# Attention and ELU network on one core: first-row products joined to the pair's run, and a wider margin in the plan's hops to TensorE

## The chip, the cores and the metric

The kernel runs on one core of a Trainium2 chip. The metric is device time in microseconds; the time before is the median of three runs. One further execution was taken with the hardware profiler, and all rows of the trace come from that one. Engines are named as in the profile: PE is TensorE (PEld its weight loads), DVE is VectorE, ACT is ScalarE, POOL is GpSimd, SP is SyncE, which issues the DMAs.

## The reference

Two stages follow each other. First causal attention for 8 batches of 8 heads, 576 rows and head size 64, with a decay bias from a running sum; then a network of two layers with an ELU between them on the 4608 rows that come out.

```python
scores = scale * q @ k.T                     # per batch and head, 576 x 576
cum = np.cumsum(np.maximum(s, 0.0), axis=-1)
bias = -(cum[:, :, :, None] - cum[:, :, None, :])
scores = np.where(causal, -1e9, scores + np.minimum(bias, 0.0))
attn = softmax(scores)                       # rows, with 1e-9 in the divisor
x = (attn @ v) as (4608, 512)
h = x @ w_in                                 # (4608, 2048)
g = np.where(h > 0.0, h, np.exp(np.minimum(h, 0.0)) - 1.0)
return g @ w_out                             # (4608, 512)
```

## The kernel before, in words

**Precision.** Most products are made from 16-bit halves: a float32 number is split into a high and a low fp16 part, and three of the four products of parts are added. The lines that make the low parts are on DVE or POOL (L1039 for values, L1255 for probabilities, L840 for x, L1676 for the hidden activations; L425 and L426 for the rest of queries and keys). Scores are made in float32 with a second product for the rest (L1176, tiles kh, qs and then k, q).

**Attention.** The rows of a batch are 64 first rows and four blocks of 128. Work goes by batch: rows 0 to 319 of batches 0 to 2 (a special path, `Low`), then batches 3 to 7 whole, then the remaining rows of batches 0 to 2. Within a batch it goes by pair of heads j = 0..3, and each head is a `Unit`. For each block of a head, a score product fills a bank of PSUM (L1176), DVE adds the mask and takes the minimum (L1179), ACT takes the exponential (L1189), and the probabilities are split into halves, written as fp16 and transposed by a DMA into the tile T (`halved`, L1211 to L1260). Batches 4 to 7 have the 64 first rows of both heads of a pair in one tile of probabilities (`early`, L1313 to L1330); their transposed form lies behind the others in T of the second head, and the first 64 values of both heads are put together by two small DMAs (L1043 to L1046).

**The products of values.** `weighing` (L1334) makes, per pair, one plan operation `heads` with 28 products (L1396) into the bank `av`, with the two heads side by side in the two halves of the array (128*64 in the profile). For the pairs with `early` there is a second operation `firsts` (L1407 to L1420) with six products of 64 columns (L1414), also in halves, into a bank `avn`. Both banks are copied to the network's input x by `produce` (L810), a high part on ACT or DVE and a low part on DVE.

**The network.** It goes by chunks of 256 rows, 18 in all. Per chunk there are eight steps; in each, `hidden` makes 24 products of 256 columns (L1636) into a bank h, ACT and DVE make the ELU and its halves (L1654 to L1676), and `project` adds 12 products of 512 columns to two sums o (L1697).

**The order.** Nothing is executed in the order of the source. Each operation is put into a `Plan` with the engines that could do it and a cost for each, a priority, and what it reads and writes. `issue` (L179) then simulates: again and again it takes the operation that can start first, and among those that can start at the same time the one with the smallest priority number; attention has small numbers, network products large ones (10000 and more), so network products fill what attention leaves of PE. The time at which an operation can start is the largest of: its engine is free; its inputs are ready plus a hop between the two engines (`ready`, L172, and the table `HOPS`, for instance 255 ns from DVE to PE and 270 from ACT to PE, 150 where the table has none, as from a DMA); and its new buffers are free (`slot_free` in `issue`, L187 to L193, the end of the last use plus 150). For work of DVE and POOL that uses memory which both read, the plan also keeps the two apart in time (`PORT_LEAD`). The plan's order becomes the program order of each engine; on the chip each engine goes through its instructions in that order and waits on semaphores where the plan's times were not met.

**Banks.** PSUM has eight banks: two for scores (tag a), one for the products of values (av), two for sums o, two for h, and one called third, which serves scores early and h later. A bank asked for by `score_bank` (L1161) belongs to tag a in the order of the source: the n-th such request gets its place in turn. A bank with the tag any and no banks of its own (as in `any_bank`, L627) takes whichever of the others it names is free.

Of the kernel before, what the change touches and what calls it, by code (L numbers as in the profile page):

```python
# [9 lines left out]
F32 = mybir.dt.float32  # L10
# [7 lines left out]
P = 128  # L18
# [9 lines left out]
N_ST, N_A, N_AV, N_H, N_O, N_IO, N_G, N_GG, N_X, N_T, N_K, N_V = 2, 2, 1, 2, 2, 2, 1, 3, 2, 2, 2, 2  # L28
# [26 lines left out]
N_FREE = 0  # L55
N_EARLY, N_AUX, N_URGENT = 2, 4, 1

FILL_T, GAP = 60e3, 350.0

N_FILL = 300  # L60
# [29 lines left out]
class Plan:  # L90
# [14 lines left out]
        ("Pool", "Pool"): 50.0,  # L105
    }
    HOP = 150.0

    BIAS = {"DVE": 1.3, "DVE-SB": 1.3}
    FIRST_BIAS = {"DVE": 1.3, "DVE-SB": 1.3}  # L110
# [21 lines left out]
    def op(self, prio, ways, reads=(), writes=(), late=()):  # L132

        o = Op()
        o.ways, o.prio, o.filler = ways, (prio, len(self.ops)), False
        o.after, o.before, o.behind, o.bufs, o.new = set(late), [], [], set(), []
        firsts = set()
        for accesses, write in ((reads, False), (writes, True)):
            for a in accesses:
                b, part = a if isinstance(a, tuple) else (a, None)  # L140
                if not b.parts and b not in o.bufs:

                    o.new.append((b, self.place(b)))
                    b.first = o
                firsts.add(b.first)
                if b not in o.bufs:
                    o.bufs.add(b)
                    b.users += 1
                for key, (writers, readers) in b.parts.items():
                    if part is None or key is None or key == part:  # L150
                        o.after.update(writers)
                        if write:
                            o.after.update(readers)
                writers, readers = b.parts.setdefault(part, ([], []))
                if write:
                    if part is None:
                        b.parts = {None: ([o], [])}
                    else:
                        b.parts[part] = ([o], [])
                else:  # L160
                    readers.append(o)
        o.after.discard(o)
        firsts -= o.after | {o}
        for d in o.after:
            d.before.append(o)
        for d in firsts:
            d.behind.append(o)
        o.left, o.ready = len(o.after) + len(firsts), {}
        self.ops.append(o)
        return o  # L170

    def ready(self, o, engine):  # L172
        return max(
            (t + (0.0 if e is None else self.HOPS.get((e, engine), self.HOP))
             for e, t in o.ready.items()),
            default=0.0,
        )

    def issue(self):  # L179
        engines = sorted({self.ENGINE.get(w[0], w[0]) for o in self.ops for w in o.ways})  # L180
        port = 0.0
        free = dict.fromkeys(engines, 0.0)
        taken = dict.fromkeys(self.tags, 0)
        slots, skipped = {}, {}
# [2 lines left out]
        def slot_free(key, bufs):  # L187

            held = slots.get(key, ())
            if len(held) < bufs:  # L190
                return 0.0
            was = held[-bufs]
            return None if was.users else was.until + self.HOP  # L193

        pending = [o for o in self.ops if not o.left]
        block = self.nc.cur_bb.bb
        last = {}
        n_done = 0
        while pending:
# [12 lines left out]
            for o in pending:  # L212
                t = 0.0
                for b, k in o.new:
# [13 lines left out]
                    t = max(t, at)  # L228
# [17 lines left out]
            engine, cost, trace = o.ways[n][:3]  # L246
            lag = 0.0
            end = start + cost
            if engine in self.PORT_LEAD:
                port = end  # L250
            engine = self.ENGINE.get(engine, engine)
# [50 lines left out]
def pe16(n):  # L302

    return n / 2.4 + 2.5
# [41 lines left out]
def kernel(  # L346
# [31 lines left out]
    HB = P // 2  # L378
# [7 lines left out]
    ps = ctx.enter_context(tc.tile_pool(name="ps", bufs=1, space=bass.MemoryType.PSUM))  # L386

    plan = Plan(tc)
    op = plan.op
# [771 lines left out]
    def score_bank(name):  # L1161

        return plan.buf(ps, [P, 512], F32, name, tag="a", bufs=N_A, others=[("third", 1, first_stage)], always=True)
# [170 lines left out]
    def weighing(u):  # L1334

        prio = u.prio + 1
        av = plan.buf(ps, [P, 512], F32, f"av_{u.tag}", tag="av", bufs=N_AV)

        def products(cost, pairs, dst, first, last):

            for m, (reads, operands) in enumerate(pairs):
                op(prio, [("PE", cost, lambda m=m, operands=operands: pe_.matmul(
                    av.v[:, dst], *operands(), start=first and m == 0,
                    stop=last and m == len(pairs) - 1))], reads, [av])

        if u.h is None:
            def pair():
                tr = plan.buf(ps, [P, 512], F32, f"tr_{u.tag}", tag="a", bufs=N_A)
                op(prio, [("PE", 111.0, lambda: pe_.transpose(tr.v[:, :P], u.pp.v, ident))],
                   [(u.pp, "data")], [tr])  # L1350
                pieces = split_pt(prio, u.tag, tr, P)
                products(pe(P), [
                    ([pc, u.vs], lambda pc=pc, m=m: (
                        u.vs.v.rearrange("p n a d -> p n (a d)")[:, 0], pc[0].v[:, m]))
                    for m, pc in enumerate(pieces)], slice(P), True, True)
                x = plan.buf(sb, [P, HB], F32, f"xs_{u.tag}", tag="xs")
                for h in range(2):
                    halves(prio, h, HB, (x, h), 0, av, h * HB)
                col = S_GROUP + 2 * groups.index((u.b, False))
                produce(prio, u.j, u.start, HB, lambda: x.v, [x, (scales, col)],  # L1360
                        lambda: scales.v[:, col : col + 1], on_psum=False)

            return [pair]

        if u.h == 0:
            return []
        pair = (u.first_head, u)
        first, last, wq = u.blocks[0], u.last + 1, P * u.n_blocks

        def columns(kb):  # L1370
            i0, half = max(kb - 1, first), kb > first
            return P * (last - i0) - HB * half

        def part(w, kb, m):
            c = columns(kb)
            if kb == last:
                return w.pt.v[:, 0, P - c :]
            end = (1 + (2 * kb + m + 1) * w.n_blocks) * P
            return w.pt.v.rearrange("p u q -> p (u q)")[:, end - c : end]

        def heads():
            terms = [(kb, m, v) for kb in range(last + 1)
                     for m, v in (((0, 0), (1, 0), (0, 1)) if kb < last else ((0, 0), (0, 1)))]
            order, rest = terms[:1], sorted(terms[1:], key=lambda t: -columns(t[0]))
            final = rest.pop(0)
            while rest:
                order.append(rest.pop())
                if rest:
                    order.append(rest.pop(0))
            order.append(final)  # L1390

            def step():
                for n, (kb, m, v) in enumerate(order):
                    dst = slice(wq - columns(kb), wq)
                    for w in pair:
                        pe_.matmul(  # L1396
                            av.v[w.h * HB : (w.h + 1) * HB, dst], w.values.v[:, w.h, kb, v], part(w, kb, m),
                            start=n == 0, stop=n == len(order) - 1,
                        )

            cost = sum((3 if kb < last else 2) * (pe16(columns(kb)) + 4) for kb in range(last + 1))
            op(prio, [("PE", 200 + cost, step)],
               [(w.pt, i) for w in pair for i in u.blocks] + [(u.values, (m, h)) for m in range(2) for h in range(2)],
               [av])
            produce(prio, u.j, u.start + HB * (first == 0), wq, lambda: av.v[:, :wq], [av], 2.0**-15)

        def firsts():  # L1407
            ends = score_bank(f"avn_{u.tag}")

            def step():  # L1410
                for n, (m, v) in enumerate(((0, 0), (1, 0), (0, 1))):
                    turned = u.pt.v[:, 1 + (u.turns[0] - 2 + m) * u.n_blocks]
                    for h in range(2):
                        pe_.matmul(  # L1414
                            ends.v[h * HB : (h + 1) * HB, :HB], u.values.v[:, 0, NQ + 1, v],
                            turned[:, h * HB : (h + 1) * HB], start=n == 0, stop=n == 2,
                        )

            op(prio, [("PE", 240.0, step)], [(u.pt, 0)] + [(u.values, ("first", h)) for h in range(2)], [ends])
            produce(prio, u.j, u.start, HB, lambda: ends.v[:, :HB], [ends], 2.0**-15)  # L1420

        return [heads] + [firsts] * u.early

    def halves(prio, h, n, dst, c0, av, a0):

# [416 lines left out]
```

## Time and profile before

| what | value |
|---|---|
| median of 3 runs | 1038.01 us (1037.63 to 1040.27) |
| profiled execution | 1035.61 us |
| its span, first to last instruction | 1033.7 us |
| granted TensorE clock | 1.000 |
| busy PE, DVE, ACT, POOL | 1014.4, 834.6, 627.0, 386.1 us |
| PE, two largest groups | L1697 378.7 us (1608 products), L1636 376.0 us (3072) |

The share of busy time says how full an engine is, not how dense: the ends of products are modelled, and a product is drawn longer than the distance to the next one. A row of the waits has the waiting engine and line, the line waited for, microseconds in total, times, and the longest. A row of the timeline has the start, the length, engine and line, what is written from what, the shape, the count, and in brackets the idle time before it and who ended it. A row of the groups has busy microseconds and the mean of one in ns behind the count. A row of the stretches has the window, its length, and busy microseconds with counts for the engines in turn.

### The profile page before, as it was taken

Reading aid. Unit: us, or ns where it says so; the run is one execution under the profiler, and the core shown is the slowest. Engines: PE = TensorE matmul, PEld = TensorE weight load, DVE = VectorE, ACT = ScalarE, POOL = GpSimd, SP = SyncE. Lnnn points to the kernel's source line nnn. Section 1 sums busy time; section 2 is a strip of 40 time slices with the busy share of each in tenths; the row PEclk is TensorE's granted clock in tenths of the full one; section 3 lists DMA queues with packets and bytes.
Section 4 is the critical chain, followed back from the end, with each engine's and each line's share of the span. In section 5 each row is a group of like instructions: output and inputs, shape, how many; then the busy total and the mean of one; then the engine's idle time right before and its main releaser. Section 6 shows DMA issues by size and latency. Waiting matters only on the chain.

```text
span 1033.7 us, 21490 instructions
## 1 busy us (share of the span) xinstructions
PE 1014.4 (98%) x7260; PEld 695.7 (67%) x7260; DVE 834.6 (81%) x2047; ACT 627.0 (61%) x1502; POOL 386.1 (37%) x605
## 2 busy tenths in 40 slices
PE   8999999999999999999999999999999999999998
PEld 6666766667676666676666666666676766676665
DVE  6889899999989999898899998888888888433333
ACT  4877756676666666766676666756666656333232
POOL 6332345464554445547556444423232322000000
PEclk9999999999999999999999999999999999999999
DMA  7767243779668677766787657747464544100000
GB/s 222 233 198 234 62 142 96 175 155 217 130 146 172 131 151 152 186 149 142 162 201 146 148 132 172 151 109 181 112 141 101 129 110 122 34 22 22 1 21 21
DMA packets 277693, 137.73 MB, mean 133 GB/s; under 512 B 211640, under 2 KB 254928, under 8 KB 277584
## 3 DMA queue, kind: packets, MB, share of 16 engines
q1 hardware_dynamic: 277584, 136.37, 54.8%
q8 instruction: 57, 0.93, 0.4%
q14 instruction: 52, 0.43, 0.1%
HBM read 68.63 MB, written 9.88 MB: 76 GB/s over the span
## 4 chain that ended last, share of the span: by engine, by line
PE 84%; DVE 9%; issue 3%; DMA 2%; ACT 1%; POOL 0%; SPq 0%; DVEq 0%; ACTq 0%; POOLq 0%
PE h L1636 30%; PE o L1697 30%; PE sc L1176 10%; PE av L1396 5%; PE o L1603 3%; PE h L1573 3%; DVE p L1255 2%; DVE v L1039 1%; DMA stk<-in_kT_dram 1%; PE trl L975 1%; PE avl L991 1%; DVE p L1179 1%; PE scratch L1760 1%; DVE g L1663 1%; DMA vs<-in_vb_dram 1%
## 5 line engine op out<-in xcount | busy, mean ns | idle before, releaser
L1697 PE MATMUL o<-wp,gg 128*128 128x512 f16 x1608 | 378.7, 380 | 1.0 <-DVE gg L1676 0.8
L1636 PE MATMUL h<-x,wp 128*128 128x256 f16 x3072 | 376.0, 273 | 0.0
L1636 PEld LDWEIGHTS <-wp 128*128 128x128 f16 x3216 | 301.8, 98 | 65.4 <-issue 8.4
L1697 PEld LDWEIGHTS <-gg 128*128 128x128 f16 x1608 | 151.3, 98 | 158.0 <-issue 3.9
L1255 DVE SCALAR_TENSOR_TENSOR p<-p,sm,p 128x512 f16<-128x512 f32 (+3 forms) x234 | 181.1, 789 | 5.3 <-POOL p L1247 2.4
L1189 ACT ACTIVATE p<-p,mn 128x192 f32<-128x192 f32 (+1 forms) x232 | 143.4, 619 | 43.8 <-DVE mn L1179 41.8
L1654 ACT ACTIVATE g<-h,cs 128x512 f32<-128x512 f32 x134 | 91.7, 684 | 111.5 <-PE h L1636 109.2
L1671 ACT ACTIVATE gg<-h,wc 128x512 f16<-128x512 f32 x122 | 83.6, 685 | 96.7 <-DVE h L1667 96.0
L1179 DVE CUSTOM_DVE_ANT_0 p<-sc,maskw 128x192 f32<-128x192 f32 (+1 forms) x232 | 109.2, 477 | 17.4 <-PE sc L1176 14.1
L1676 DVE SCALAR_TENSOR_TENSOR gg<-h,wc,gg 128x512 f16<-128x512 f32 x134 | 99.8, 745 | 25.8 <-ACT gg L1671 25.1
L1176 PE MATMUL sc<-kh,qs 128*128 128x192 f32 (+2 forms) x272 | 109.1, 405 | 7.0 <-DVE mn L1179 5.6
L1247 POOL TENSOR_SCALAR p<-p,sm 128x512 f16<-128x512 f32 (+3 forms) x105 | 61.1, 586 | 145.4 <-DVE sm L1198 104.0
L1667 DVE SCALAR_TENSOR_TENSOR h<-g,cs,h 128x512 f32<-128x512 f32 x134 | 100.6, 751 | 16.2 <-ACT g L1659 12.1
L1663 DVE TENSOR_SCALAR g<-g 128x512 f32<-128x512 f32 x77 | 37.2, 483 | 74.4 <-ACT g L1654 74.1
L1251 ACT ACTIVATE p<-p,sm 128x512 f16<-128x512 f32 (+3 forms) x114 | 67.6, 603 | 32.4 <-DVE sm L1198 30.9
L1176 PE MATMUL sc<-k,q 128*128 128x192 f32 (+2 forms) x272 | 83.2, 309 | 0.0
L1176 PEld LDWEIGHTS sc<-kh,qs 128*128 128x128 f32 x272 | 51.4, 189 | 28.4 <-DVE mn L1179 7.3
L426 POOL TENSOR_TENSOR qs<-stq,qs 64x512 fp32r<-64x512 f32 (+1 forms) x53 | 63.5, 1198 | 6.7 <-ACT qs L407 1.2
L426 POOL TENSOR_TENSOR k<-stk,kh 64x576 fp32r<-64x576 f32 x36 | 54.8, 1523 | 15.3 <-ACT kh L407 11.8
L1396 PE MATMUL av<-T,v 128*64 128x256 f16 (+5 forms) x896 | 60.3, 286 | 0.0
L405 POOL TENSOR_SCALAR qs<-stq 128x512 fp32r<-128x512 f32 (+1 forms) x42 | 27.9, 664 | 72.9 <-DMA stq<-in_qT_dram 51.6
L1176 PEld LDWEIGHTS sc<-k,q 128*128 128x128 f32 x272 | 51.8, 190 | 1.9
(216 smaller groups left out, 1326.1 us busy)
## 6 DMA issues: line engine op xcount, KB each, us to landing
stk<-in_kT_dram SPq DMA_DIRECT2D x64, 288.0 KB
va<-in_vb_dram SPq DMA_DIRECT2D x32, 320.0 KB
stq<-in_qT_dram SPq DMA_DIRECT2D x40, 256.0 KB
w_raw<-in_w_in_dram SPq DMA_DIRECT2D x16, 512.0 KB
w_raw<-in_w_out_dram SPq DMA_DIRECT2D x16, 512.0 KB
out_dram<-ost SPq DMA_DIRECT2D x32, 256.0 KB
q<-qs SPq DMA_DIRECT2D x40, 128.0 KB
T<-p SPq DMA_TRANSPOSE x208
```

Source lines behind the costliest of these rows:

```text
L426: ("Pool", pool_2(n), lambda: pool.tensor_tensor(dst(), src(), hi(), ALU.subtract)),
L1176: pe_.matmul(view(sc.v[:, :cw]), l, r, start=n == 0, stop=n == len(pairs) - 1)
L1179: op(prio, [("DVE", 84 + dve_p(cw), lambda i=i, sc=sc: dve.tensor_tensor_reduce(pt.v[:, i * cw : (i + 1) * cw], sc.v[:, :cw], mv(i * cw, c ...
L1189: op(prio, [("ACT", 480 + w / 1.2, lambda: act.activation(pt.v[:, :w], pt.v[:, :w], AF.Exp, bias=mn.v[:, at : at + 1], scale=-1.0, accum_o ...
L1255: ("DVE-SB", dve_2(n), lambda part=part: dve.scalar_tensor_tensor(part(t16, 1), own(part), by(part), part(t16, 0), ALU.mult, ALU.subtract)),
L1396: pe_.matmul(av.v[w.h * HB : (w.h + 1) * HB, dst], w.values.v[:, w.h, kb, v], part(w, kb, m), start=n == 0, stop=n == len(order) - 1,)
L1636: pe_.matmul(hp.v[:, m], weight_part(f, 0, part)[1]()[:, c * P : (c + 1) * P], x.v[:, xx, c, o : o + TC], start=(c == 0 and i == 0), stop= ...
L1654: op(side, [("ACT", act_c(2 * TC) + 90, lambda: act.activation(gt.v, flat(hp.v), AF.Exp, scale=by(BACK)))], [hp, (cs[ch], g)], [gt])
L1667: op(side, [("DVE", dve_b(2 * TC), lambda: dve.scalar_tensor_tensor(flat(hp.v), gt.v, by(MINUS if sign[0] else FIRST), flat(hp.v), ALU.mul ...
L1671: ("ACT", act_c(2 * TC) + 90, lambda: act.activation(flat(gg.v[:, 0]), flat(hp.v), AF.Copy, scale=down())),
L1676: op(side, [("DVE", dve_b(2 * TC), lambda: dve.scalar_tensor_tensor(flat(gg.v[:, 1]), flat(hp.v), down(), flat(gg.v[:, 0]), ALU.mult, ALU. ...
L1697: pe_.matmul(acc[i].v, gg.v[:, a, m, i * P : (i + 1) * P], weight_part(2 * fp + m, 1, part)[1](), start=(first and m == 0 and k == 0), sto ...
```

## The change

Two things are changed. `firsts` is no operation of its own any more: for the pairs that have it, its six products are the first products of the operation `heads`, which now also reads the first values and opens the bank `ends`; the plan's cost goes from 200 to 350 ns more than the sum of its products. The bank `ends` is asked for with the tag any, and so takes a score bank when one is free, outside the order of the tag a. The other change is in the plan: once its time for PE is past 250e3 ns, `more()` adds 800 ns to each hop from another engine to PE in `ready`, and to the release of every buffer, for any engine, in `slot_free`.

```diff
+MORE_T = 250e3
...
+    MORE = 800.0
...
     def ready(self, o, engine):
+        more = self.more() if engine == "PE" else 0.0
         return max(
-            (t + (0.0 if e is None else self.HOPS.get((e, engine), self.HOP))
+            (t + (0.0 if e is None else self.HOPS.get((e, engine), self.HOP) + more * (e != "PE"))
              for e, t in o.ready.items()),
             default=0.0,
         )
 
+    def more(self):
+        return self.MORE if self.now > MORE_T else 0.0
...
-            return None if was.users else was.until + self.HOP
+            return None if was.users else was.until + self.HOP + self.more()
...
-        def firsts():
-            ends = score_bank(f"avn_{u.tag}")
-
-            def step():
+            def first_rows():
                 for n, (m, v) in enumerate(((0, 0), (1, 0), (0, 1))):
...
-            op(prio, [("PE", 240.0, step)], [(u.pt, 0)] + [(u.values, ("first", h)) for h in range(2)], [ends])
-            produce(prio, u.j, u.start, HB, lambda: ends.v[:, :HB], [ends], 2.0**-15)
-
-        return [heads] + [firsts] * u.early
+            cost = sum((3 if kb < last else 2) * (pe16(columns(kb)) + 4) for kb in range(last + 1))
+            reads = [(w.pt, i) for w in pair for i in u.blocks]
+            reads += [(u.values, (m, h)) for m in range(2) for h in range(2)]
+            if not u.early:
+                op(prio, [("PE", 200 + cost, step)], reads, [av])
+            else:
+                ends = plan.buf(ps, [P, 512], F32, f"avn_{u.tag}", tag="any", bufs=0, others=[("a", N_A)], always=True)
+                op(prio, [("PE", 350 + cost, lambda: (first_rows(), step()))],
+                   reads + [(u.values, ("first", h)) for h in range(2)], [av, ends])
+                produce(prio, u.j, u.start, HB, lambda: ends.v[:, :HB], [ends], 2.0**-15)
+            produce(prio, u.j, u.start + HB * (first == 0), wq, lambda: av.v[:, :wq], [av], 2.0**-15)
+
+        return [heads]
```

More of the change, by code (lines that the diff above doesn't have):

```diff
@@ L177, in ready @@
         )
+    def more(self):
+        return self.MORE if self.now > MORE_T else 0.0
     def issue(self):
         engines = sorted({self.ENGINE.get(w[0], w[0]) for o in self.ops for w in o.ways})
-        port = 0.0
+        port = self.now = 0.0
         free = dict.fromkeys(engines, 0.0)
@@ L1399, in step @@
                         )
[L1401 to L1405, printed above, removed]
-        def firsts():
-            ends = score_bank(f"avn_{u.tag}")
-            def step():
+            def first_rows():
                 for n, (m, v) in enumerate(((0, 0), (1, 0), (0, 1))):
```

## The prediction

> **What bounds the kernel now.** I read the page first, its busy table and its forty slices.
>
> ```profile
> span 1033.7 us, 21490 instructions
> PE 1014.4 (98%) x7260; PEld 695.7 (67%) x7260; DVE 834.6 (81%) x2047; ACT 627.0 (61%) x1502; POOL 386.1 (37%) x605
> ...
> PE   8999999999999999999999999999999999999998
> ...
> DVE  6889899999989999898899998888888888433333
> ```
>
> TensorE is busy from end to end, so only what TensorE itself saves can move the end. VectorE is nearly full while attention and network run together and half empty in the last six slices, where only the network is left. Next come the stretches. The columns after the window are the busy microseconds of PE, PEld, DVE, ACT and POOL.
>
> ```profile
> 250.00:900.00 650.00, 641.82 (x4883) 440.51 (x4881) 563.55 (x1387) 414.25 (x990) 274.24 (x398) 1.00 0.63 142
> 900.00:1025.00 125.00, 125.00 (x866) 84.54 (x865) 45.75 (x70) 39.65 (x60) 0.00 (x0) 1.00 0.04 14
> ```
>
> Behind 900 us PE has no gap at all. Between 250 and 900 us, the stretch that the change's threshold (250e3 ns of the plan's own time) opens, PE has 650.0 - 641.8 = 8.2 us of visible gaps. The waits of that stretch name them.
>
> ```profile
> PE sc L1176 <- DVE mn L1179: 5.6, 9, 1.3
> PE sc L1176 <- DVE x L840: 1.3, 1, 1.3
> PE o L1697 <- DVE gg L1676: 0.8, 1, 0.8
> PE peaks L649 <- DVE tops L641: 0.3, 1, 0.3
> ```
>
> Twelve waits, 5.6 + 1.3 + 0.8 + 0.3 = 8.0 us, all for VectorE, and ten of them are a score product that waits until VectorE has read an older score bank. This is not the whole price, because the end of a product in the trace is modelled and lies behind the start of the next one:
>
> ```profile
> L1636 PE MATMUL h<-x,wp 128*128 128x256 f16 x3072 | 376.0, 273 | 0.0
> ...
> 947.34 5.24 PE h L1636 x48
> ```
>
> One hidden product is drawn 0.273 us long, but in a dense run 48 of them take 5.24 us, 0.109 us each. A wait must therefore first use up 0.273 - 0.109 = 0.16 us before a gap shows. Twelve waits hide another 12 x 0.16 = 1.9 us, so waits for other engines cost about 10 us in this stretch, some 1% of the span. That is all the wider margin can win.
>
> **The change, first part: the sixteen separate visits for the first rows.** The products of `firsts` use two halves of the array (128*64), as those of `heads` do; everything around them uses the whole array (128*128). The timeline of PE shows what such a visit costs.
>
> ```profile
> L1414 PE MATMUL avn<-T,v 128*64 128x64 f16 x96 | 4.5, 203 | 0.0
> ...
> 437.44 1.04 PE L1697 MATMUL o<-wp,gg 128*128 128x512 f16 x4 [0.83 <-DVE gg L1676]
> 438.41 0.28 PE L1414 MATMUL avn<-T,v 128*64 128x64 f16 x6
> 438.62 0.47 PE L1176 MATMUL sc<-kh,qs 128*128 128x448 f32 x1
> 438.93 0.37 PE L1176 MATMUL sc<-k,q 128*128 128x448 f32 x1
> 439.14 1.47 PE L1697 MATMUL o<-wp,gg 128*128 128x512 f16 x6
> 440.44 1.15 PE L1636 MATMUL h<-x,wp 128*128 128x256 f16 x9
> 441.34 0.38 PE L1176 MATMUL sc<-kh,qs 128*128 128x288 f32 x1
> 441.56 0.29 PE L1176 MATMUL sc<-k,q 128*128 128x288 f32 x1
> 441.69 0.30 PE L1176 MATMUL sc<-kh,qs 128*128 128x288 f32 x1
> 441.82 0.29 PE L1176 MATMUL sc<-k,q 128*128 128x288 f32 x1
> 441.96 1.81 PE L1636 MATMUL h<-x,wp 128*128 128x256 f16 x15
> ```
>
> There are 96 / 6 = 16 visits. The `o` product takes (440.44 - 439.14) / 6 = 0.217 us. Four of them from 437.44 end at 438.31, and the next `o` starts at 439.14, so visit and score pair together take 0.83 us. A score pair without a visit: nine `h` from 440.44 end at 441.42, the next `h` starts at 441.96, so two pairs of 288 columns take 0.54 us, 0.47 ns per column and product. The pair of 448 columns is thus worth 2 x 448 x 0.47 = 0.42 us, and 0.83 - 0.42 = 0.41 us is the visit. Its own work is three pairs of 64 columns side by side, at 0.217 / 512 us a column 3 x 0.027 = 0.08 us. So 0.33 us is the way into the half-array form and out of it. One visit had hidden products behind it instead of scores:
>
> ```profile
> 461.95 1.36 PE L1636 MATMUL h<-x,wp 128*128 128x256 f16 x11
> 463.24 0.28 PE L1414 MATMUL avn<-T,v 128*64 128x64 f16 x6
> 463.46 0.83 PE L1636 MATMUL h<-x,wp 128*128 128x256 f16 x6
> ```
>
> Eleven `h` end at 463.15, the next starts at 463.46: 0.31 us, of it 0.23 us of way in and out. In the timeline of all sixteen, fifteen have a score pair right behind. Inside the run of `heads` the six products need no way of their own, since that run pays it already. So the merge saves 15 x 0.33 + 0.23 = 5.2 us, at least 16 x 0.23 = 3.7 us if scores come to stand behind the longer run more often than now. It adds no product, no copy and no DMA. What it adds is conditions: the run now also waits for the two small copies of the first values and for a free score bank, and holds that bank about 2 us longer. Neither is a wait on PE if the plan knows of it, since the plan puts network products first. If the cover failed, one such wait costs what a score wait costs, up to 1.5 us.
>
> **Second part: 800 ns more from other engines to PE, and on every reuse of a buffer, in the plan.** This changes no instruction, only the order. A score pair that the plan thought ready at T is now put on PE at T + 800 or later, and network products go ahead of it. To see what that is worth, take one of the long waits, with VectorE's and GpSimd's rows.
>
> ```profile
> 498.80 2.72 DVE L1039 SCALAR_TENSOR_TENSOR v<-va,scales,v 128x320 f16<-128x320 f32 x2
> ...
> 501.44 0.61 DVE L1179 CUSTOM_DVE_ANT_0 p<-sc,maskw 128x448 f32<-128x448 f32 x1
> ...
> 499.63 1.53 POOL L426 TENSOR_TENSOR k<-stk,kh 64x576 fp32r<-64x576 f32 x1
> ...
> 502.11 0.40 PE L1176 MATMUL sc<-kh,qs 128*128 128x288 f32 x1 [1.27 <-DVE mn L1179]
> ...
> L1039 DVE SCALAR_TENSOR_TENSOR v<-va,scales,v x47: 536/594/1691, 273.5 to 866.8; 128x320 f16<-128x320 f32 x47
> ```
>
> Two L1039 took 2.72 us where twice the median is 2 x 0.594 = 1.19 us: VectorE came 1.5 us late while GpSimd's L426 ran beside it, the score reduction queued behind came late by that, and PE waited 1.27 + 0.16 = 1.43 us. The lateness is VectorE's, and a margin of 0.8 us on PE does not remove it; it covers 0.8 of the 1.43. The Trainium skill (SBUF — State Buffer, section Who interferes with whom) goes further: a VectorE instruction with two SBUF inputs and a GpSimd instruction that reads SBUF exclude each other for the whole of the instruction that came first. By that rule such collisions stay as long as they are however PE is ordered, and the margin would win at most 0.8 us from each; the stretch from 1.19 to 2.72 us agrees with it in kind.
>
> Of the waits, 0.8 us goes from each, or the whole where it is shorter. In the timeline four are about as long as the longest shown, 1.3 + 0.16 = 1.46 us, with 0.66 left each, and the `o` wait at 0.99 with 0.19 left: 4 x 0.66 + 0.2 = 2.8 us left, and 10 - 2.8 = 7 us gone. Bounds: 10 us if all go, and a loss of the same size if the new order brings as many waits again. I take 5.8 us: nearer to the 7, because the wait of the row above is of the kind that the 0.8 shortens, and a little under it, because a new order will have some stalls of its own. Who pays for the later scores: the score banks stand free longer, and attention may fall behind; network products fill PE meanwhile, as they do in the stretch behind 900 us with no gap.
>
> Sum: 5.2 + 5.8 = 11.0 us. The profiled execution took 1035.6 us (span 1033.7 and 1.9 around it), which would become 1024.6. The median of the runs lies 2.4 us above the profiled one, so for it 1038.0 - 11.0 = 1027.0 us. A measurement of this kernel can tell about 0.3%, 3.1 us, from no change.
>
> **Rivals.** First, only the merge works: VectorE's lateness is not noise around the plan but accumulates, PE catches up with it whatever head start it gives, and the waits come back at the same sum. For it speaks that the four long waits are all past 0.8 us; against it, that VectorE has 650 - 563.6 = 86 us idle in the stretch to recover in. Time: 1038.0 - 5.2 = 1032.8 us.
>
> Second, slower: new collisions. The margin is also on every buffer's release, so the plan puts work of ScalarE, VectorE and GpSimd up to 0.8 us later than it can really start. They run ahead of the plan, and GpSimd's L426 meets VectorE's instructions where the plan had held them apart.
>
> ```profile
> L1255 DVE SCALAR_TENSOR_TENSOR p<-p,sm,p x203: 268/742/1894, 254.4 to 891.3; 128x512 f16<-128x512 f32 x58, 128x256 f16<-128x256 f32 x16, 128x384 f16<-128x384 f32 x14, 128x64 f16<-128x64 f32 x14
> ```
>
> L1255 shows the size: up to 1.89 us, 1.15 above its median. The place is 375 to 650 us, where the long waits are. It decides when the waits grow by more than the merge's 5.2 us, that is by four waits of 1.46 us; if they double, 10 - 5.2 = 4.8 us is lost: 1042.8 us. Against it: the margin itself covers 0.8 of each.
>
> Third, the gains cancel: the merged run's added conditions hold it and the scores behind it, and some four waits of 1.3 us eat the merge while the margin wins nothing: 1038.0 us.
>
> Fourth, attention becomes the bound and the network runs out of rows.
>
> ```profile
> L1176 PE MATMUL sc<-kh,qs x233: 252/392/559, 250.5 to 880.8; 128*128 128x288 f32 x57, 128*128 128x448 f32 x28, 128*128 128x320 f32 x16, 128*128 128x192 f32 x16
> ...
> 900.00:1033.70 133.70, 66.64 (x576) 0.00 (x0) 36.91 (x49) 32.64 (x49) 1.00 0.05 17
> ```
>
> The second row is the tile h alone: 576 products, three chunks of 192, are still to do when attention is over, some 130 us. If every one of the 233 score pairs lost 0.8 us on its bank, two banks would lose 233 x 0.8 / 2 = 93 us. That is less than the cushion, so this needs a second delay; I give it no time of its own beyond the second rival's and put it with it.
>
> **How the numbers follow.** Both parts work: 0.60, 1027.0 us, between 1021 and 1031. Only the merge: 0.17, 1032.8 us. Cancelled: 0.10, 1038.0. Slower by new waits or by starving: 0.13, 1042.8. Faster by over 0.3% takes the first two less a hundredth: 0.76; within 0.3% gets that and the third: 0.11; slower 0.13. The range goes down to all waits gone with the merge at its best and 2 us for fewer score pairs behind half-array runs, 1038 - 5.2 - 10 - 2 = 1021, and up to 1037, which leaves out the slower case and part of the cancelled one.
>
> **What would show it.** Right: the first-row products follow or precede `av` products with no whole-array product between them, and visits into the half-array form between 250 and 900 us fall from 45 to 29; PE's gaps there fall from 8.2 to about 3 us; the waits of scores for L1179 fall from nine to four or fewer, each under 0.7 us; the last score pair starts between 880 and 920 us. The order up to about 250 us stays as it is. Wrong: gaps of PE at 8 us or more, above all with more long L1255 or L1039 rows at them; a network product that waits for an `x` tile; or half-array visits as many as before.

## The result and the profile after

| | before | after |
|---|---|---|
| median | 1037.82 us (1035.50 to 1040.27, 4 runs) | 1020.55 us (1019.64 to 1022.21, 4 runs) |
| profiled execution, span | 1035.61, 1033.7 us | 1020.64, 1018.7 us |
| ratio, 95% interval | | 0.9835 (0.9809 to 0.9861) |

The changed kernel is 17.3 us faster where 11.0 were forecast, and 1020.55 lies just under the low end of the range, 1021.0. The direction was right, the size was not. In the new file the line numbers of the score part are higher by 8 (L1176 is L1184, L1179 is L1187, L1255 is L1263); the value products are L1404 and the first-row products L1413.

The page of the changed kernel, with the busy table and the chain by engine:

```profile
span 1018.7 us, 21522 instructions
PE 1006.9 (99%) x7260; PEld 696.9 (68%) x7260; DVE 817.3 (80%) x2044; ACT 618.8 (61%) x1497; POOL 396.3 (39%) x607
...
PE 90%; DVE 4%; DMA 2%; issue 2%; SPq 1%; ACT 0%; POOL 0%; DVEq 0%; ACTq 0%; POOLq 0%
```

PE makes the same 7260 products in 15 us less span. On the chain VectorE has 4%; the same line of the page before is

```profile
PE 84%; DVE 9%; issue 3%; DMA 2%; ACT 1%; POOL 0%; SPq 0%; DVEq 0%; ACTq 0%; POOLq 0%
```

The stretches after (busy PE, PEld, DVE, ACT, POOL behind the window's length):

```profile
0.00:250.00 250.00, 243.05 (x1499) 169.22 (x1500) 223.19 (x588) 173.67 (x456) 110.73 (x205) 1.00 0.62 171
250.00:900.00 650.00, 649.79 (x4987) 451.78 (x4987) 549.40 (x1387) 413.11 (x995) 285.59 (x402) 1.00 0.64 144
```

Between 250 and 900 us PE's gaps fell from 8.2 to 0.2 us, and 4987 products start there instead of 4883. The view of PE's waits for this window has no row left; before it had four. Ahead of 250 us nothing was won: the order of PE first differs at 238 us.

Here is one of the sixteen runs that now begin with the first rows:

```profile
338.81 1.67 PE L1705 MATMUL o<-wp,gg 128*128 128x512 f16 x7
340.41 0.28 PE L1413 MATMUL avn<-T,v 128*64 128x64 f16 x6
340.53 2.10 PE L1404 MATMUL av<-T,v 128*64 128x512 f16 x28
342.56 0.42 PE L1184 MATMUL sc<-kh,qs 128*128 128x320 f32 x1
342.81 0.31 PE L1184 MATMUL sc<-k,q 128*128 128x320 f32 x1
342.96 0.28 PE L1644 MATMUL h<-x,wp 128*128 128x256 f16 x1
```

The six products need 340.53 - 340.41 = 0.12 us and have no way in or out of their own; before, a visit took 0.31 to 0.41 us. And here is a place where VectorE comes late and PE does not notice, from the timelines of VectorE, GpSimd and PE:

```profile
452.25 2.20 DVE L1047 SCALAR_TENSOR_TENSOR v<-va,scales,v 128x320 f16<-128x320 f32 x2
454.38 0.74 DVE L1263 SCALAR_TENSOR_TENSOR p<-p,sm,p 128x512 f16<-128x512 f32 x1
...
455.12 0.47 DVE L1187 CUSTOM_DVE_ANT_0 p<-sc,maskw 128x320 f32<-128x320 f32 x1
...
452.24 1.40 POOL L434 TENSOR_TENSOR k<-stk,kh 64x576 fp32r<-64x576 f32 x1
...
453.65 0.45 PE L1184 MATMUL sc<-kh,qs 128*128 128x448 f32 x1
453.94 0.37 PE L1184 MATMUL sc<-k,q 128*128 128x448 f32 x1
454.15 2.76 PE L1705 MATMUL o<-wp,gg 128*128 128x512 f16 x12
456.56 0.48 PE L1184 MATMUL sc<-kh,qs 128*128 128x288 f32 x1
```

The two value splits (L1047) took 2.20 us beside GpSimd's L434, where two at the median of this line, 0.545 us, take 1.09, as at 498 us before. But the next score pair that needs a bank stands behind a whole group of 12 network products, and the bank was read by 455.6, about 1 us ahead of it.

For the tables below I also worked out waits that the gaps hide: from the starts of the products in the timeline, each distance between network products less what the products in between take in dense runs, and less the usual way into and out of the half-array form; what is left over 60 ns counts as a wait. By that, the kernel before has 18 waits with 12.3 us between 250 and 900 us, and the changed one 3 with 1.1 us. These figures depend a little on what is taken as dense, by some tenths of a microsecond and a few short waits in each run.

### The profile page after: what moved, and what is told of

It is laid out like the page before. It is cut to its first block, busy times and chain, and to the rows that moved or that the text cites. A ratio compares the mean times of both kernels' runs of the same rounds, so it can differ in the third digit from the quotient of the medians.

```text
span 1018.7 us, 21522 instructions
## 1 busy us (share of the span) xinstructions
PE 1006.9 (99%) x7260; PEld 696.9 (68%) x7260; DVE 817.3 (80%) x2044; ACT 618.8 (61%) x1497; POOL 396.3 (39%) x607
## 4 chain that ended last, share of the span: by engine, by line
PE 90%; DVE 4%; DMA 2%; issue 2%; SPq 1%; ACT 0%; POOL 0%; DVEq 0%; ACTq 0%; POOLq 0%
PE o L1705 33%; PE h L1644 33%; PE sc L1184 10%; PE av L1404 5%; PE o L1611 3%; PE h L1581 3%; PE trl L983 1%; PE avl L999 1%; DVE p L1263 1%; SPq L401 1%; DMA kl<-in_kT_dram 1%; DMA vs<-in_vb_dram 0%; DMA w_raw<-in_w_out_dram 0%; DMA aux_dram<-aux 0%; PE sc_n L1330 0%
## 5 line engine op out<-in xcount | busy, mean ns | idle before, releaser
L1263 DVE SCALAR_TENSOR_TENSOR p<-p,sm,p 128x512 f16<-128x512 f32 (+3 forms) x237 | 173.4, 747 | 8.3 <-POOL p L1255 5.4
L1255 POOL TENSOR_SCALAR p<-p,sm 128x512 f16<-128x512 f32 (+3 forms) x130 | 83.6, 648 | 183.7 <-DVE sm L1206 154.6
L1187 DVE CUSTOM_DVE_ANT_0 p<-sc,maskw 128x192 f32<-128x192 f32 (+1 forms) x232 | 109.2, 478 | 23.1 <-PE sc L1184 21.8
L1184 PE MATMUL sc<-kh,qs 128*128 128x192 f32 (+2 forms) x272 | 112.8, 417 | 0.2
L1184 PE MATMUL sc<-k,q 128*128 128x192 f32 (+2 forms) x272 | 83.0, 309 | 0.0
L1259 ACT ACTIVATE p<-p,sm 128x512 f16<-128x512 f32 (+3 forms) x95 | 56.6, 603 | 34.9 <-DVE sm L1206 30.4
L1184 PEld LDWEIGHTS sc<-kh,qs 128*128 128x128 f32 x272 | 51.5, 189 | 20.0 <-issue 3.7
L434 POOL TENSOR_TENSOR qs<-stq,qs 64x512 fp32r<-64x512 f32 (+1 forms) x50 | 59.8, 1196 | 12.6 <-ACT qs L415 5.9
L1404 PE MATMUL av<-T,v 128*64 128x256 f16 (+5 forms) x896 | 60.2, 285 | 0.0
L434 POOL TENSOR_TENSOR k<-stk,kh 64x576 fp32r<-64x576 f32 x34 | 51.2, 1506 | 18.1 <-ACT kh L415 15.3
L1184 PEld LDWEIGHTS sc<-k,q 128*128 128x128 f32 x272 | 51.9, 191 | 2.6
L1404 PEld LDWEIGHTS <-v 128*64 128x64 f16 x896 | 40.1, 110 | 14.8 <-issue 4.9
```

Of the source, the lines that this page charges most:

```text
L434: ("Pool", pool_2(n), lambda: pool.tensor_tensor(dst(), src(), hi(), ALU.subtract)),
L1184: pe_.matmul(view(sc.v[:, :cw]), l, r, start=n == 0, stop=n == len(pairs) - 1)
L1187: op(prio, [("DVE", 84 + dve_p(cw), lambda i=i, sc=sc: dve.tensor_tensor_reduce(pt.v[:, i * cw : (i + 1) * cw], sc.v[:, :cw], mv(i * cw, c ...
L1263: ("DVE-SB", dve_2(n), lambda part=part: dve.scalar_tensor_tensor(part(t16, 1), own(part), by(part), part(t16, 0), ALU.mult, ALU.subtract)),
L1404: pe_.matmul(av.v[w.h * HB : (w.h + 1) * HB, dst], w.values.v[:, w.h, kb, v], part(w, kb, m), start=n == 0, stop=n == len(order) - 1,)
```

## The experiments

All ratios are against the kernel before on the same chip, with 95% intervals; the clock granted was 0.996 to 1.000 in every run. PE busy and waits are of the stretch from 250 to 900 us in the profiled execution of each.

| run | median us | ratio | PE busy of 650 us | waits, us (count) |
|---|---|---|---|---|
| before | 1036.55, 1037.10, 1037.34 (beside e1 to e4, e5 to e8, e9 to e11) | | 641.82 | 12.3 (18) |
| changed | 1020.55 | 0.9835 (0.9809 to 0.9861) | 649.79 | 1.1 (3) |
| e1, merge only | 1031.19 | 0.9942 (0.9927 to 0.9956) | 642.71 | 11.9 (22) |
| e2, margin only | 1025.60 | 0.9891 (0.9873 to 0.9908) | 649.87 | 0.8 (2) |
| e3, hops only | 1029.90 | 0.9936 (0.9920 to 0.9951) | 646.54 | 8.7 (25) |
| e4, release only | 1020.19 | 0.9834 (0.9818 to 0.9850) | 649.94 | 0.3 (1) |
| e5, score banks only | 1021.09 | 0.9845 (0.9831 to 0.9858) | 647.91 | 3.1 (5) |
| e6, 400 ns | 1022.01 | 0.9864 (0.9844 to 0.9885) | 646.52 | 7.0 (13) |
| e7, 1600 ns | 1021.46 | 0.9840 (0.9824 to 0.9857) | 650.00 | 0.4 (2) |
| e8, from the start | 1027.32 | 0.9904 (0.9890 to 0.9917) | 648.46 | 2.6 (5) |
| e9, before, no separation | 1057.86 | 1.0194 (1.0180 to 1.0208) | 635.19 | 23.8 (40) |
| e10, changed, no separation | 1041.82 | 1.0041 (1.0026 to 1.0056) | 643.46 | 13.1 (26) |
| e11, 1200 ns from 170 us | 1018.50 | 0.9820 (0.9806 to 0.9835) | 650.00 | 0.0 |

**The two parts alone.** The first question was whether the two parts bring their gains apart. The merge alone has the margin at zero:

```diff
-    MORE = 800.0
+    MORE = 0.0
```

> The merge alone, the margin set to 0. Theory A (two separate gains: the merge takes away sixteen ways into and out of the half-array form, the margin covers VectorE's lateness): half-array visits fall by 16, worth 4.7 us by the two traces, and PE's waits for VectorE stay at some 10 us; 5 us faster than before, ratio 0.995. Rival C (the waits came from the separate operation, whose score bank was bound to its place in the order of the banks): the waits go with the merge; 12 us or more faster, ratio 0.988.

The margin alone is the kernel before with the lines of `ready`, `more` and `slot_free` of the change.

> The margin alone, on the kernel before with its separate first-row operations. Theory A: 48 half-array visits as before, the waits for VectorE almost gone; 10 us faster, ratio 0.990. Rival C: the waits stay, 5 us or less faster, ratio 0.995.

Both came out by theory A. Visits into the half-array form between 250 and 900 us are 29 in e1 and 45 in e2, as in the kernel before (the expectation has 48 for that). The merge alone wins 0.58% (6.0 us of 1036.55, interval 4.6 to 7.6), the margin alone 1.09% (11.3 us, 9.5 to 13.2), and 0.9942 x 0.9891 = 0.9834 is the ratio of both together. So they add up, and rival C falls: with the merge alone the waits stay. PE's waits in e1 show one thing more:

```profile
PE sc L1184 <- DVE mn L1187: 3.1, 7, 0.8
PE avn L1413 <- DVE mn L1187: 2.5, 3, 1.2
PE h L1644 <- DVE gg L1684: 0.8, 1, 0.8
```

Three of the joined runs wait for a score bank, 2.5 us together. This is the added condition that the prediction named (its third rival); it is real, and the margin covers it, since the changed kernel has no such row.

**Which half of the margin.** Hops to PE alone, and release of buffers alone, both with the merge:

```diff
-            return None if was.users else was.until + self.HOP + self.more()
+            return None if was.users else was.until + self.HOP
```

> The changed kernel with the margin on the hops to PE alone, none on the release of buffers. Nearly all waits of the kernel before are scores that wait for L1179 to have read an older score bank, which is a release and not a hop. Theory A therefore expects the waits to stay at 8 us or more: 5 to 7 us faster than before, ratio 0.994. If the hops matter, the waits are gone and it is as fast as the changed kernel, ratio 0.984.

```diff
-            (t + (0.0 if e is None else self.HOPS.get((e, engine), self.HOP) + more * (e != "PE"))
+            (t + (0.0 if e is None else self.HOPS.get((e, engine), self.HOP))
```

> The changed kernel with the margin on the release of buffers alone, none on the hops to PE. Theory A: as fast as the changed kernel within 2 us, ratio 0.985 to 0.987, with waits of scores for L1179 under 2 us in all. If the hops matter as much, the waits are half of before: ratio 0.990.

The hops bring nothing that can be measured beside the merge (0.9936 against 0.9942), though waits in their trace are a little shorter, and the release brings all of it. The next run narrows it to the two score banks:

```diff
-            return None if was.users else was.until + self.HOP + self.more()
+            return None if was.users else was.until + self.HOP + self.more() * (key[1] == "a")
```

with the hops as in e4.

> The changed kernel with the margin on the release of the two score banks alone: no other bank, no buffer in SBUF, no hop. Theory A1 (the waits are scores that come too early for the bank that VectorE still reads): as fast as the changed kernel within 3 us, ratio 0.984 to 0.987, waits of scores under 2 us. Rival (the release of buffers in SBUF reorders ScalarE, VectorE, GpSimd and the DMAs, and that makes the difference): the waits stay above 5 us, ratio 0.992.

With the two score banks alone the gain is there within the interval, 0.9845 against 0.9834. What is left is mostly a single wait of another bank, and nothing of it concerns SBUF:

```profile
PE h L1644 <- DVE gg L1684: 1.4, 1, 1.4
PE sc L1184 <- DVE mn L1187: 0.7, 2, 0.4
```

**The size.** 

```diff
-    MORE = 800.0
+    MORE = 400.0
```

> The changed kernel with 400 instead of 800 ns. The rule of the prediction (each wait is shortened by the margin and no more): the waits of the merge alone, 22 of some 12 us in all, keep 12 - 22 x 0.4 at the most, 4 to 6 us; ratio 0.988. Rival (the later place also lies behind whole network products, so more than the margin is covered): 1 to 3 us of waits left, ratio 0.985 to 0.986.

The ratio, 0.9864, lies between what the two expected, and its interval holds both; the waits of the profiled execution, 7.0 us, lie above both, but that execution took 1027.1 us, 5 us over the median of its kernel. That 400 ns covers only a part is seen in that one execution; by the medians it is not shown, since the interval overlaps that of 800 ns. With `MORE = 1600.0`:

> The changed kernel with 1600 instead of 800 ns. If 800 already covers all waits: as fast as the changed kernel, ratio 0.983 to 0.985, since the 130 us of network behind the last scores hide a slower attention. If attention becomes the bound: the last scores come later than 1000 us and the time rises above 1025 us, ratio over 0.988.

No gap of PE is left (650.00 of 650 us), and the time is that of the changed kernel. Attention is indeed slower; its last score product starts at 914 us, 50 us later than that of the changed kernel, and the network behind it hides that. First the changed kernel, then e7:

```profile
863.90 0.29 PE L1184 MATMUL sc<-k,q 128*128 128x288 f32 x1
...
914.23 0.29 PE L1184 MATMUL sc<-k,q 128*128 128x288 f32 x1
```

**The place.** With `MORE_T = 0.0`:

> The changed kernel with the margin from the start and not from 250e3 ns. Theory A: ahead of 170 us there are too few network products to put ahead of a score, PE must wait for the chain of attention anyway, and a margin only sends the chain through later: no gain, within 3 us of the changed kernel or slower by up to 10, ratio 0.983 to 0.995. Rival: the waits of the first stage are lateness too and go: 5 us or more faster than the changed kernel, ratio 0.979 or less.

By the two ratios (0.9904 and 0.9835) it is about 7 us slower than the changed kernel, in the way that theory A described. PE's groups show where most of it went: into filler products (L1768, an identity turned over so that PE is not idle), which the plan puts where it finds nothing else in the first 60 us. In e8 they are

```profile
L1768 PE MATMUL scratch<-ident 128*128 128x128 f32 x138 | 20.4, 293 | 0.0
```

and in the changed kernel

```profile
L1768 PE MATMUL scratch<-ident 128*128 128x128 f32 x86 | 14.4, 314 | 0.0
```

52 more at the dense distance of 0.109 us are 5.7 us, which is most of the difference. In the first 60 us only 39 products of the network are made in the changed kernel, and 32 in e8: there is little to put ahead of a score, and the margin becomes idle time.

**The source of the lateness.** To see whether the waits come from VectorE meeting GpSimd, the plan's separation of the two was taken away, in both kernels:

```diff
-    PORT_LEAD = {"DVE-SB": 240.0, "Pool": 120.0}
+    PORT_LEAD = {}
```

> The kernel before with the plan's separation of VectorE and GpSimd (PORT_LEAD) emptied, so that the two meet more often. Theory (the waits are VectorE's lateness from meeting GpSimd): VectorE's busy time between 250 and 900 us grows by 15 us or more, PE's waits there from 12 to 18 us or more; 5 to 15 us slower than before, ratio 1.005 to 1.015. If the lateness has another source: busy time and waits as before, ratio 1.000.

> The changed kernel with the same separation emptied. Theory (the margin does not stop the meetings, it covers the lateness): VectorE's busy time grows as in the run beside it, but PE's waits between 250 and 900 us stay under 5 us; within 8 us of the changed kernel, of which what lies ahead of 250 us is shared with the run beside it, ratio 0.985 to 0.992. If the margin worked by fewer meetings: the waits come back, ratio over 0.995.

The first 250 us of the kernel before, then the two stretches of the same kernel without the separation:

```profile
0.00:250.00 250.00, 243.50 (x1498) 169.02 (x1499) 224.32 (x589) 172.12 (x452) 111.89 (x208) 1.00 0.62 172
...
0.00:250.00 250.00, 236.78 (x1424) 162.14 (x1426) 221.03 (x562) 163.91 (x435) 122.24 (x221) 1.00 0.60 169
250.00:900.00 650.00, 635.19 (x4791) 430.74 (x4785) 578.42 (x1399) 389.67 (x938) 345.67 (x472) 1.00 0.64 144
```

Between 250 and 900 us VectorE is busy 14.9 us longer (578.4 against 563.6), and the waits double, from 12.3 to 23.8 us. That fits lateness from such meetings, but the plan also gave GpSimd more work (345.7 us against 274.2), so it is no pure test. The time rose by more than expected (ratio 1.0194, not up to 1.015), and part of that was lost ahead of 250 us, where 1424 products start instead of 1498. The expectation for e10 failed: its waits are 13.1 us and not under 5, and its ratio, 1.0041, lies where the rival (fewer meetings) had put it. It is 16.0 us faster than e9, nearly the 17.3 us by which the changed kernel beats the one before. The change thus takes away about 11 us of waits in either case (23.8 - 13.1 = 10.7, 12.3 - 1.1 = 11.2), and where there is twice the lateness the rest stays.

So e10 leaves the rival standing. It is answered by e4, whose VectorE rows have instructions as stretched as before while PE is busy 649.94 of 650 us:

```profile
L1263 DVE SCALAR_TENSOR_TENSOR p<-p,sm,p x201: 268/745/1897, 253.4 to 868.0; 128x512 f16<-128x512 f32 x58, 128x384 f16<-128x384 f32 x17, 128x256 f16<-128x256 f32 x14, 128x64 f16<-128x64 f32 x12
L1047 DVE SCALAR_TENSOR_TENSOR v<-va,scales,v x51: 532/547/1694, 251.0 to 846.2; 128x320 f16<-128x320 f32 x51
```

The longest are 1.90 and 1.69 us, before 1.89 and 1.69. The longest alone do not say how many there are. So here is a count, for each trace, of all VectorE instructions between 250 and 900 us that took over 0.8 us more than the fastest tenth of the same operation, tiles and shape in all thirteen traces; I take such an instruction as a sign of a meeting.

| | before | changed | e1 | e3 | e4 | e11 | e9 | e10 |
|---|---|---|---|---|---|---|---|---|
| stretched instructions | 28 | 21 | 30 | 24 | 25 | 30 | 39 | 44 |
| PE's waits, us | 12.3 | 1.1 | 11.9 | 8.7 | 0.3 | 0.0 | 23.8 | 13.1 |

The runs e3 and e4 have as many stretched instructions, and 8.7 and 0.3 us of waits; e11 has about as many as the kernel before, and no wait. Fewer meetings are thus not what took the waits away. In e9 and e10, where the separation is gone, there are 11 and 23 more than in the same kernel with it.

**A faster version.** The last run has 1200 ns from 170 us on:

```diff
-MORE_T = 250e3
+MORE_T = 170e3
...
-    MORE = 800.0
+    MORE = 1200.0
```

> The changed kernel with a margin of 1200 ns from 170e3 ns on, an attempt at a faster version: behind 250 us the changed kernel has 1.1 us of waits left, between 170 and 250 us about 1 us. Theory: at most 2 us to win, ratio 0.981 to 0.984. If the network at 170 to 250 us has too few products to put ahead: slower than the changed kernel, ratio over 0.986.

It has no wait left behind 250 us and the lowest median of all, 1018.50 us. Its interval (0.9806 to 0.9835) overlaps that of the changed kernel, so 1 to 2 us better is likely and not shown.

## Why the prediction was wrong in size

**The bound held.** PE sets the end, and what was won are PE's waits and its ways into and out of the half-array form. Less work on another engine alone moved nothing: in e1 VectorE is busy 551.2 us in the stretch instead of 563.6, and PE's waits stay at 11.9 us.

**The merge** was forecast at 5.2 us, at least 3.7; alone it measured 6.0 (4.6 to 7.6). The half-array visits fell from 45 to 29, as said. The Trainium skill (TensorEngine Tiling (Array Packing), section Key Properties) states that a change of the tiling mode drains TensorE; the 0.23 and 0.33 us around six products agree with a price per change and not per product, since the six add only about 0.1 us inside the run of `heads`.

**The margin** was forecast at 5.8 us and measured 11.3 (9.5 to 13.2). This is the step that failed, in three places of the same sum. First, "waits for other engines cost about 10 us": I added 0.16 us to each of the twelve gaps that show. That is right between two network products, but a score product starts 0.03 us behind the start of a network product in dense runs, so more is hidden: the waits that show as 1.27 us at 502.11 and 1.30 us at 489.33 are 1.52 and 1.65 us by the starts. And waits under some 0.3 us leave almost no gap or none, since the product before is drawn over them. By the starts there are 18 waits with 12.3 us. Second, "2.8 us left": 0.8 us was to go from each wait, and four long ones were to keep 0.66 us each. In the changed kernel 1.1 us is left in all, none over 0.62. By the starts that rule would leave 3.2 of the 12.3 us of the kernel before, and 1.3 of the 11.9 of the merge alone; e2, the margin on the kernel before, has 0.8 us left. So the rule did not hold there. Why stays open: a score does not move by 0.8 us but behind whole network products, as at 454.15 above, and the new order also has other meetings; e6, which was to test the first, did not decide it. Third, the step from 7 down to 5.8 "because a new order will have some stalls of its own" had no row behind it; the 1.1 us left are all the stalls that came. The low end of the range went wrong with the first: it took 10 us as all that could go.

**The rivals.** That only the merge works is refuted by e2. That lateness accumulates, its reason, is not seen in the changed kernel; in e10, where VectorE has twice as many stretched instructions, 13.1 us of waits come past the margin, but whether they accumulate was not tested. New collisions did not decide: VectorE's busy time fell by 14.2 us (563.6 to 549.4). The Trainium skill (SBUF — State Buffer, section Who interferes with whom) states that a VectorE instruction with two SBUF inputs contends with a GpSimd instruction that reads SBUF; the long rows of e4 agree. From that I took that the margin can win at most 0.8 us from each meeting, and e2 did not bear this out. Cancelled gains: the wait that this rival named exists in e1, at 2.5 us, and is covered. Starving: e7 delays attention by 50 us and loses nothing, so the cushion was real.

**Other signs that I gave.** The waits of scores were to fall from nine to four or fewer: none shows. The last score pair was to start between 880 and 920 us and came at 863.9. I had the sign of that wrong for the merge: the merge alone ends attention at 845.7 us instead of 881.2, and the margin alone at 880.5. In the kernel before, the bank of the first rows was bound to its turn among the score banks, so scores behind it had to wait for it in the plan; taking any free bank lifts that. This reading is argued from the source and these three times, and was not tried by itself.

## What to carry to other kernels

In an order planned ahead, a busy engine's waits on one whose times vary can be covered by slack at the point where the two meet, here the release of two PSUM banks, as long as there is independent work to put in between; where there is none, the same slack is idle time. Measure the waits of a pipelined engine from start to start and not by its gaps, which hide the short ones. Small products in another array form belong beside others of that form.

## What the runs showed of the hardware

A change from the whole-array form into the half-array form and back cost TensorE 0.23 us when 16-bit products followed and 0.33 us when a float32 score pair did, for short and long runs alike. By the medians of the starts, the six products take 0.31 and 0.41 us, of which 0.08 us are their columns. The run of 28 products of 64 to 512 columns takes 2.15 and 2.25 us, of which 4544 columns (two products side by side) at the 0.217 / 512 us of an `o` product are 1.92 us. A score pair between 16-bit products takes 0.21, 0.27, 0.30 and 0.41 us for 192, 288, 320 and 448 columns.

The value split on VectorE (L1039 before, two inputs of 128x320) has a median of 0.54 to 0.60 us in the thirteen traces, and its longest are 1.69 to 1.79 us. Each one of over 1.0 us ran beside a two-input instruction of GpSimd; others beside such an instruction stayed short.
